# A state-space scan beside dilated attention on one core: output rows in pairs, the scan's weights built in pieces on two engines, K's weights loaded in halves, and a new written-out order

## The chip, the cores and the metric

The kernel runs on one core of a Trainium2 chip. A core has TensorE (PE; its weight loads are listed apart, as PEld), VectorE (DVE), ScalarE (ACT), GpSimd (POOL) and SyncE (SP), which here issues nearly all DMAs. The metric is the device time of one execution in microseconds, the median of several runs. Beside it stands one execution taken by the profiler, with its own time and its span from the first to the last instruction.

## The reference

Two independent parts work on inputs of 2048 tokens by 448 features in bf16, and their results are joined along the features to 2048 by 896. Cut to what is computed:

```
# part A: a diagonal linear recurrence (state-space layer), complex state of P = 448
Lam_bar = exp(exp(log_dt) * Lam);  B_bar = ((Lam_bar - 1) / Lam)[:, None] * Bmat
Bu = einsum("bld,pd->blp", x, B_bar)
h_t = Lam_bar * h_(t-1) + Bu_t                       # 2048 steps
y = 2 * einsum("blp,dp->bld", h, Cmat).real + x * Dskip
# part B: 16 heads of 28; each query sees 8 keys, 2 tokens apart, back in time
qkv = x @ wqkv
attn = softmax(q . k[pos - 2 w] * 28**-0.5, w = 0..7, masked before the start)
b = (sum_w attn_w * v[pos - 2 w]) @ wo
return concatenate([y, b], axis=-1)
```

## The kernel before, in words

**Layout.** A token is t = 16 p + j: p (0 to 127) is the partition or the column of a tile, j (0 to 15) picks the tile. All inputs x are brought in transposed by DMA (line 361 for part B, in `load_x` for part A), except that B's tokens 12 to 15 come plainly and are transposed by TensorE (`prep`, line 426), to have work early.

**Part B.** `prep` projects Q and K (lines 476 to 509) and evicts them from PSUM, `qk` multiplies q and shifted k on VectorE (lines 649 to 655) and sums heads on TensorE with 0/1 matrices (lines 666 and 672), `softmax` takes maximum, exponential, sum and normalizes. `v_proj` makes V (lines 755 and 762), whose evictions go to ScalarE (line 214) or VectorE (line 218). `pv` multiplies V by the attention and sums on VectorE in four groups of four tokens (lines 817, 820, 829, 832), then transposes and multiplies by wo (lines 857 to 900). For the last group (tokens 0 to 3) the sum of two halves is not made by VectorE: line 869 transposes both halves into one PSUM tile, 8 matmuls a token, and adds them there.

**Part A.** The state is handled as 7 blocks m of 64 complex entries. For each block `powers` builds 15 powers of the recurrence's 2x2 rotations as 128x128 matrices on VectorE (line 1182, one instruction of 128x1920). `scan` runs the recurrence of a block as a tree: first matmuls of x (lines 1232 and 1241) into four PSUM banks, ScalarE casts them to SBUF (L1250 or L1253), a matmul by a power adds them to the next bank (L1256), cast (L1260), and so on down to 64 columns (casts L1284, matmuls L1287 to L1294), then back up (L1301 to L1339). Each step of a block is a matmul that waits for a cast of ScalarE, and a cast that waits for a matmul; several blocks are interleaved. The carries of lines 1307 and 1308 are two matmuls each, of 128 and of 384 columns, since the last quarter of the state lies in a tile of its own. `outputs` gives y by seven matmuls a token over the blocks (line 1434), after four with Dskip (line 1430) for tokens 0 to 11; for tokens 12 to 15 VectorE multiplies x by Dskip (line 1411) and adds it in the eviction (line 1446).

**PSUM.** A pair of banks has the tag "W", six single banks the tag "s"; a matmul group that wants a bank waits until an eviction has freed it.

**The order.** Each step is a unit that is added to a `Planner` with its engine or a choice of two, a cost, and the units that it needs. If a list `ORDER` of the right length is there, the units are issued in just that order: an entry is the unit's number, and 1000 more when the second of its two engines is to do it. So the engine of each eviction, and the order on every engine, is written out by hand in that list; the costs only serve a search of it. Engines work strictly in their own order.

**DMA.** SP issues the loads in the order of the list: x of tokens 12 to 15 (line 345), K's weights (lines 338 and 340: rows 64 to 447, then the first 64 rows), Q's weights the same way, then the transposes. Output rows leave one token at a time (line 910 for attention, line 1449 for the state-space part), 32 transfers of 112 KB; rows for part B have four buffers (`yb`), those for part A eight (`ya`).

Of the kernel before, what the change touches and what calls it, by code (L numbers as in the profile page):

```python
# [9 lines left out]
ACT = mybir.ActivationFunctionType  # L10
# [22 lines left out]
QW = 2 + NCH  # L33
LV2 = ((1, 2, 3), (4, 8, 12), (16, 32, 48))
KPOW = sorted({1, 2, 4, 8, 12, 16} | {32 * k for ks in LV2 for k in ks})
# [5 lines left out]
FILL = (1, 3)  # L41
# [4 lines left out]
YG = ((3,), (7,), (11,), (1, 5), (9,), (0, 4), (8,), (2, 6), (10,), (12, 13), (14,), (15,))  # L46
YSPLIT = 8
ORDER = [
# [156 lines left out]
class Ctx:  # L205
# [83 lines left out]
    def warm(self):  # L289
# [5 lines left out]
        nc.vector.memset(z, 0.0)  # L295
        box = {}
# [10 lines left out]
    def late_tile(self):  # L307
        if self.late is None:
            self.late = self.rc
            self.ya_v = self.late[:, 8448:8448 + 3584].rearrange("p (r d) -> p r d", r=8)  # L310
            self.yb_v = self.late[:, 12032:12032 + 1792].rearrange("p (r d) -> p r d", r=4)
            self.ya_ring, self.yb_ring, self.ya_row = Ring(8), Ring(4), {}
        return self.late


class PartB:
# [7 lines left out]
    def loads(self):  # L324
# [11 lines left out]
        def wload(c0, c1):  # L336
            w = self.wqk[:, :, c0:c1] if c0 < 2 * D else self.wv
            nc.sync.dma_start(w[:, 1:4], self.B_wqkv[DT:D, c0:c1].rearrange("(k p) c -> p k c", p=NCH))
            for rows in ((slice(DT, NCH),) if c0 < 2 * D else (slice(0, DT), slice(DT, NCH))):
                nc.sync.dma_start(w[rows, 0], self.B_wqkv[0:DT, c0:c1])  # L340
        self.wload = wload
# [4 lines left out]
        wload(D, 2 * D)  # L346
        self.u_x3 = [P.add("ACTQ", 0.0, lambda: None, lat=t) for t in (3.45, 3.95)]
        self.u_w["K"] = P.add("ACTQ", 0.0, lambda: None, lat=6.2)

    def loads_more(self):  # L350
# [16 lines left out]
        u0 = self.u0 = P.add("SP", 2.35, lambda: None, lat=0.0)  # L367
        self.u_w["Q"] = P.add("SP", 1.0, lambda: self.wload(0, D), [u0], -1, lat=4.4)
# [8 lines left out]
    def load_v(self, deps):  # L377
        self.u_w[2] = self.plan.add("SP", 1.2, lambda: self.wload(2 * D, 3 * D), deps, 0.5, lat=3.5)
# [32 lines left out]
    def prep(self, u_warm):  # L411
# [6 lines left out]
        def xpose(j):  # L418
            box = {}

            def tr():
                pt = box["pt"] = self.psum.tile([NCH, 2, KT, NCH], bf16, name="pt_x", tag="s")
                for n in range(2):
# [3 lines left out]
            u = P.add("PE", 0.9, tr, [self.u_x3[(j - 12) // 2]], -8.5, acq="s")  # L427
# [24 lines left out]
        def banks(b, r, tiles, boxes, prio, rfirst):  # L452
# [5 lines left out]
            for kind, kt in tiles:  # L458
                wd.append(self.u_wm if kind == "M" else self.u_w[kind])
# [1111 lines left out]
```

## Time and profile before

| | us |
|---|---|
| median of 3 runs (lowest, highest) | 140.3 (139.42, 140.81) |
| the profiled execution's own time | 140.44 |
| its span | 138.7 |
| busy: TensorE, VectorE, ScalarE, GpSimd | 131.6, 123.8, 90.0, 17.7 |
| transfers of output rows | 32 of 112 KB, 1.8 from issue to landing (median) |
| granted clock of TensorE | 1.000 |

A row of the groups has the line, the engine, the operation, what it writes and reads, the shapes and the count, then the busy time and the mean duration in ns of one, then the idle time of the engine before them and what ended it. A row of a timeline has start, duration and the same names. A matmul's duration includes its way through the array; neighbours overlap, so what one costs is read from start to start. ScalarE's and VectorE's instructions overlap with the next one by about a tenth of a microsecond in the same way.

### The profile page before, as it was taken

How to read it: one execution, taken by the hardware profiler on the slowest of the kernel's cores; microseconds unless marked ns; L12 is line 12 of the kernel's file. 1: busy time of each engine (PE TensorE's matmuls, PEld its weight loads, DVE VectorE, ACT ScalarE, POOL GpSimd, SP SyncE). 2: the span in 40 equal slices, each digit the busy share in tenths (PEclk: the TensorE clock that was granted, in tenths of full speed). 3: DMA queues.
4: the chain of work that ended last, by engine and by line, in shares of the span. 5: the costliest groups of instructions: out<-in, count | busy, mean ns of one | idle time of the engine just before them, and what ended most of it. 6: DMA issues, size and time to landing. Idle time of an engine off the chain costs nothing.

```text
span 138.7 us, 2854 instructions
## 1 busy us (share of the span) xinstructions
PE 131.6 (95%) x1078; PEld 68.5 (49%) x1085; DVE 123.8 (89%) x136; ACT 90.0 (65%) x202; POOL 17.7 (13%) x69
## 2 busy tenths in 40 slices
PE   5999999999999999999999999999999999988990
PEld 1634435444555554756435564545655554534640
DVE  2268999899999999999999999999999999999820
ACT  3464589997563967776685998987637070722671
POOL 7489820028000000000000000000000000000000
PEclk9999999999999999999999999999999999999999
DMA  4979943645653349735898019000000827965774
GB/s 128 266 128 213 173 87 63 160 101 116 80 111 74 82 84 145 140 81 150 230 185 195 0 25 112 0 0 2 5 0 0 183 82 43 213 211 155 234 233 139
DMA packets 39582, 16.05 MB, mean 116 GB/s; under 512 B 31573, under 2 KB 38932, under 8 KB 39569
## 3 DMA queue, kind: packets, MB, share of 16 engines
q1 hardware_dynamic: 39506, 15.87, 54.0%
q8 instruction: 8, 0.13, 0.4%
q14 instruction: 5, 0.04, 0.1%
q10 hardware_dynamic: 63, 0.01, 0.0%
HBM read 4.32 MB, written 3.67 MB: 58 GB/s over the span
## 4 chain that ended last, share of the span: by engine, by line
DVE 35%; PE 31%; SPq 15%; issue 7%; DMA 6%; ACT 3%; DVEq 0%; ACTq 0%
DVE rb L820 13%; DVE prods L817 11%; SPq L361 8%; PE v_ps L762 7%; DVE rb L817 4%; PE qk_ps L476 4%; DMA out_dram<-qk 3%; PE logits L666 3%; PE y_ps L1434 3%; DMA rb<-in_B_x_dram 3%; DVE pw L1182 2%; DVE rb L829 2%; PE wo_ps L900 2%; PE scb L1232 2%; PE scp L1232 2%
## 5 line engine op out<-in xcount | busy, mean ns | idle before, releaser
L817 DVE TENSOR_TENSOR prods<-attn,vd 128x3584 bf16<-128x3584 bf16 x12 | 24.1, 2019 | 0.0
L820 DVE TENSOR_TENSOR rb<-rb,prods 128x3584 bf16<-128x3584 bf16 x11 | 22.2, 2021 | 0.1
L651 DVE TENSOR_TENSOR prods<-qk 128x3072 bf16<-128x3072 bf16 (+1 forms) x15 | 19.1, 1327 | 0.0
L214 ACT CAST qk<-wo_ps 128x448 bf16<-128x448 f32 (+1 forms) x16 | 8.3, 527 | 12.2 <-PE wo_ps L893 7.7
L1434 PE MATMUL y_ps<-Ccat,qk 128*128 128x448 bf16 x60 | 15.1, 352 | 0.1
L476 PE MATMUL qk_ps<-rb 128*128 128x512 bf16 x60 | 14.4, 379 | 0.0
L1434 PE MATMUL y_ps<-Ccat,h 128*128 128x448 bf16 x45 | 11.0, 352 | 0.9 <-ACT qk L214 0.9
L214 ACT CAST vd<-v_ps 128x448 bf16<-128x448 f32 x15 | 7.4, 539 | 5.8 <-PE v_ps L762 4.5
L1232 PE MATMUL scb<-xaT_sb,Bcat 128*128 128x512 bf16 x42 | 10.9, 380 | 0.0
L1232 PEld LDWEIGHTS <-Bcat 128*128 128x128 bf16 x84 | 7.6, 100 | 6.6 <-issue 0.4
L1284 ACT CAST ubuf<-scb 128x64 bf16<-128x64 f32 x35 | 7.1, 218 | 5.6 <-PE scb L1291 3.5
L762 PE MATMUL v_ps<-rb 128*128 128x448 bf16 x48 | 9.9, 353 | 0.0
L655 DVE TENSOR_TENSOR prods<-qk 128x768 bf16<-128x768 bf16 (+3 forms) x18 | 9.1, 569 | 0.3 <-ACT qk L214 0.2
L216 ACT ACTIVATE qk<-qk_ps 64x512 bf16<-64x512 f32 (+1 forms) x15 | 8.9, 599 | 0.6 <-PE qk_ps L509 0.3
L476 PEld LDWEIGHTS <-rb 128*128 128x128 bf16 x60 | 5.6, 98 | 7.1 <-DMA rb<-in_B_wqkv_dram 0.5
L1434 PEld LDWEIGHTS <-qk 128*128 128x128 bf16 x60 | 5.9, 98 | 5.3
L817 DVE TENSOR_TENSOR rb<-attn,vd 128x3584 bf16<-128x3584 bf16 x4 | 8.1, 2022 | 0.1
L893 PE MATMUL wo_ps<-wo_p,rb 128*128 128x448 bf16 x36 | 8.1, 354 | 0.0
L1182 DVE TENSOR_TENSOR pw<-Dm,spair 128x1920 bf16<-128x1920 bf16 x7 | 8.1, 1153 | 0.0
L214 ACT CAST qk<-qk_ps 128x512 bf16<-128x512 f32 (+2 forms) x11 | 6.3, 585 | 2.6 <-PE qk_ps L483 1.1
L1232 PE MATMUL scp<-xaT_sb,Bcat 128*128 128x512 bf16 x30 | 7.8, 380 | 0.0
L666 PE MATMUL logits<-prods,Zsel 128*32 128x256 bf16 x192 | 7.4, 274 | 0.0
(199 smaller groups left out, 261.9 us busy)
## 6 DMA issues: line engine op xcount, KB each, us to landing
out_dram<-qk SPq DMA_DIRECT2D x32, 112.0 KB, 1.8
vd<-vd SPq DMA_DIRECT2D x3, 392.0 KB, 4.7
rb<-in_B_wqkv_dram SPq DMA_DIRECT2D x3, 336.0 KB, 5.0
qk<-in_A_x_dram SPq DMA_DIRECT2D x1, 448.0 KB
ra<-in_A_B_re_dram SPq DMA_DIRECT2D x1, 392.0 KB, 4.3
ra<-in_A_B_im_dram SPq DMA_DIRECT2D x1, 392.0 KB, 5.9
rb<-in_A_C_re_dram SPq DMA_DIRECT2D x4, 98.0 KB, 2.9
rb<-in_A_C_im_dram SPq DMA_DIRECT2D x4, 98.0 KB, 2.8
```

Of the source, the lines that this page charges most:

```text
L214: nc.scalar.copy(out, in_)
L361: nc.sync.dma_start(self.xT[:, j], bass.AP(x.tensor, x.offset + j * D - DT, [[T * D, NCH], [1, KT * NCH]]), transpose=True)
L476: nc.tensor.matmul(out(n), lhsT=w(n, full, k), rhs=self.xT[:, j:j + 4, k, :], start=(not rfirst and k == 1), stop=(rfirst and k == KT - 1) ...
L651: V.tensor_tensor(out.rearrange("p i j k q -> p i (j k) q"), qq.unsqueeze(1).to_broadcast([NCH, 2, 4 * nk, NCH]), bass.AP(kk.tensor, kk.of ...
L655: V.tensor_tensor(jk(out[:, i, a:e]), qq, kk, op=ALU.mult)
L666: nc.tensor.matmul(lg[32 * i:32 * i + 32, 2 * tp:2 * tp + 2, :], lhsT=cx.Z[:, kt, zs], rhs=pr[:, :, i, kt, :], start=(new and kt == 0), st ...
L762: nc.tensor.matmul(box["ps"][:].rearrange("p h d -> p (h d)"), lhsT=self.xT[:, j, k, :], rhs=self.wv[:, k, :], start=False, stop=(k == KT ...
L817: V.tensor_tensor(tmp[i].rearrange("p (j d h) -> p j d h", j=8, d=DH), aa, self.vd[:, o:o + 8], op=ALU.mult)
L820: V.tensor_tensor(acc, acc, tmp[i], op=ALU.add)
L1182: V.tensor_tensor(t[:], self.o["Dm"][:].rearrange("p (a b) -> p a b", b=2).unsqueeze(1).to_broadcast([NCH, 2 * NPW, 32, 2]), self.sp[:, m ...
L1232: mt(box[i], lhsT=self.Bcat[:, k, m, :], rhs=self.xk(slice(i, None, 4), k), start=(i % 2 == 0 and k == 0), stop=False, **kw)
L1434: nc.tensor.matmul(ps, lhsT=h, rhs=self.Ccat[:, m, :], start=(m == 0 and not skip), stop=(m == NM - 1), skip_group_check=True)
```

## The change

1. *Powers in pieces.* The 15 powers of a block are built in four pieces (3, 4, 4 and 4 powers), each by VectorE in one instruction or by ScalarE in one ACTIVATE for each half of a power (128x64, the scale read per partition from a new f32 copy of the factors, which GpSimd makes). The scan's steps wait for their piece and not for all 15.
2. *Last sums joined by VectorE.* After each half of the last attention sum VectorE adds its two halves (128x896), and the transposes of tokens 0 to 3 are 4 matmuls each instead of 8.
3. *Output in pairs.* The 16 state-space rows leave in 8 transfers of two tokens, the attention rows of tokens 4 to 15 in 6; tokens 0 to 3 leave alone. Attention rows have six buffers. An attention pair is evicted in two casts behind each other. For tokens 0 to 3 the eviction can be ScalarE's or VectorE's.
4. *K's weights in halves.* The columns of K come in two transfers (256 and 192 columns, rows 64 to 447); the first 64 rows of K and Q together in one, issued by ScalarE. The first group of K's matmuls (tokens 12 to 15) is done in halves of two tokens as they come. Tokens 14 and 15 are transposed apart, and the warm-up has two matmuls less.
5. *Carries in one.* The tiles of the state are laid out so that the last quarter lies beside the others (132 columns each), and a carry is one matmul of 512 columns.
6. *The order.* 715 units instead of 687, in a new order, with other choices of engine.

The diff, cut to its core (the list to the lines that hold the first power pieces):

```diff
-FILL = (1, 3)
+FILL = (1, 1)
+PCUT = ((0, 3), (3, 7), (7, 11), (11, 15))
+MERGE = 1
+ADD = (0,0,0,0,0,0,0)
+OUTP = ((1, 5), (2, 6), (0, 4), (12, 13), (7, 11), (8, 9), (3, 10), (14, 15))
...
+    87, 88, 1079, 1093, 178, 1084, 138, 188, 179, 181, 273, 34, 1161, 1231, 97, 98, 110, 111, 112, 99, 102, 180,
...
+    127, 136, 128, 129, 175, 1125, 190, 196, 132, 546, 521, 522, 547, 549, 524, 186, 1233, 1357, 134, 548, 523, 550,
+    525, 133, 183, 187, 516, 541, 536, 542, 544, 537, 539, 517, 519, 191, 137, 184, 193, 1520, 1518, 1232, 1276,
+    1275, 545, 538, 540, 543, 185, 194, 192, 551, 531, 526, 552, 213, 527, 554, 529, 205, 214, 215, 553, 1315, 555,
...
-        wload(D, 2 * D)
+        for c0, c1 in ((D, D + 256), (D + 256, 2 * D)):
+            nc.sync.dma_start(self.wqk[:, 1:4, c0:c1], self.B_wqkv[DT:D, c0:c1].rearrange("(k p) c -> p k c", p=NCH))
...
+        nc.scalar.dma_start(self.wqk[DT:NCH, 0], self.B_wqkv[0:DT, 0:2 * D])
...
                         V.tensor_tensor(a, a, t, op=ALU.add)
+                        if MERGE:
+                            V.tensor_tensor(a[:, 0], a[:, 0], a[:, 1], op=ALU.add)
...
-                    for y in range(2):
+                    for y in range(2 - MERGE):
...
-                nc.sync.dma_start(self.out_b[:, j, :], cx.yb_v[:, jb["y"]])
+                if g:
+                    a, b = jb["mate"]["y"], jb["y"]
+                    nc.sync.dma_start(self.out_b[:, j - 1:j + 1, :], cx.yb_v[:, a:b + 1:b - a])
...
-        u = P.add("DVE", vec2(2 * NPW * PL), build, [self.u_s, *deps], prio, acq="pw")
+            n = 2 * (b - a)
+            if eng == "ACT":
+                for i in range(2 * a, 2 * b):
+                    nc.scalar.activation(t[:, i].rearrange("p a b -> p (a b)"), self.o["Dm"][:], ACT.Copy,
+                                         scale=self.spf[:, 2 * m * NPW + i:2 * m * NPW + i + 1])
+            else:
+                V.tensor_tensor(t[:, 2 * a:2 * b], self.o["Dm"][:].rearrange("p (a b) -> p a b", b=2).unsqueeze(1).to_broadcast(
+                    [NCH, n, 32, 2]),
...
+            us.append(P.add(("DVE", "ACT"), (vec2(n * PL), n * act(PL)), lambda eng, a=a, b=b: build(eng, a, b),
+                            [self.u_s, self.u_sf, *deps, *us[:1]], prio, acq=None if a else "pw"))
...
-            def carry(out, lt, Sc, hv):
-                mt(out[:, 0:NCH], lhsT=lt, rhs=Sc, start=False, stop=True, **kw)
-                mt(out[:, NCH:512], lhsT=lt, rhs=hv[:, 3, 0:384], start=False, stop=True, **kw)
...
+                mt(box[1].rearrange("p (g c) -> p g c", g=4), lhsT=L(2), rhs=hget()[1][:, :, 2:2 + NCH],
+                   start=False, stop=True, **kw)
...
-                nc.sync.dma_start(self.out_a[:, j, :], cx.ya_v[:, cx.ya_row[j]])
+                nc.sync.dma_start(self.out_a[:, a:b + 1:b - a, :], cx.ya_v[:, rows[a]:rows[b] + 1:rows[b] - rows[a]])
```

How the new list reads for what follows. The pieces of block m are units 231 to 234 (m = 0), 273 to 276 (1), 315 to 318 (2), 357 to 360 (3), 395 to 398 (4), 437 to 440 (5) and 477 to 480 (6). With 1000 more, so on ScalarE, stand 1231, 1232, 1233, 1274, 1275, 1276, 1315, 1316, 1317, 1357, 1358, 1360, 1395, 1477 and 1478; the other 13 are VectorE's. Those that begin a block (1231, 1315, 1357, 1395, 1477) are three powers, so 6 ACTIVATEs, the others 8.

ScalarE's own order from about the first piece to the scan's first cast is: piece 0 of block 0; the evictions of K and Q and of B's weights; pieces 2 of block 0 and 0 of block 3; two Q evictions with V of tokens 3, 10, 2 and 11 between them; pieces 1 of block 0, 3 and 2 of block 1; V of tokens 4, 7, 6, 5 and 1; piece 0 of block 2; V 0 and 12, the exponential, V 13, a copy; piece 1 of block 3; V 14; piece 1 of block 1; then the scan's first cast (L1253). Inside the scan stand 1316 (ahead of the 256-column cast of block 1), 1317, 1360 (ahead of that of block 2), 1395, 1477 and 1478.

In this stretch ten evictions and copies change from ScalarE to VectorE (a copy of B's weights, one of x, one Q and one K tile of 128 rows, one K tile of 64 rows, two tiles of the state's input weights, V of tokens 8, 9 and 15) and three from VectorE to ScalarE (a K tile of each half, V of token 1). Ahead of it three evictions of 64 rows go to VectorE and four of 128 rows to ScalarE. TensorE's order up to the scan's first dependent matmul has one group of three matmuls of block 1 behind it that was ahead of it.

More of the change, by code (lines that the diff above doesn't have):

```diff
@@ L295, in warm @@
         nc.vector.memset(z, 0.0)
+        self.first = self.pool.tile([NCH, 2], f32, name="first")
+        nc.vector.memset(self.first[:, 0:1], 0.0)
         box = {}
@@ L416, in prep, with xpose @@
         sc = DH ** -0.5
-        def xpose(j):
+        def xpose(j, nt):
             box = {}
             def tr():
-                pt = box["pt"] = self.psum.tile([NCH, 2, KT, NCH], bf16, name="pt_x", tag="s")
-                for n in range(2):
+                pt = box["pt"] = self.psum.tile([NCH, nt, KT, NCH], bf16, name="pt_x", tag="s")
+                for n in range(nt):
                     for k in range(KT):
@@ L491, in banks @@
                 res = ua, ub
+            elif j == 12 and tiles[0][0] == "K":
+                us = []
+                for a in (0, 2):
+                    for n in range(2):
+                        us.append(P.add("PE", pe(3, 256), lambda n=n, a=a: f(n, a, a + 2), x[a:a + 2] + wd + us[-1:], prio, acq=None if a else "s"))
+                u = P.add("PE", pe(1, 512), rr, [us[-1]] + dup, prio, mode="r")
+                us.append(u)
+                res = u, u
             else:
@@ L1327, in back, with fresh, s6, s7 @@
                 mt(box[2 * n], lhsT=cx.ident[:], rhs=box["eP"][:, n, :], start=True, stop=False, **kw)
[L1329 to L1333 removed]
+            def fresh(n, box=box, pair=pair):
+                if pair and n == 0:
+                    t = box["P"] = self.psum.tile([NCH, 2, 512], f32, name="scP", tag="W")
+                    box[0], box[2] = t[:, 0, :], t[:, 1, :]
+                elif not pair:
+                    box[2 * n] = self.psum.tile([NCH, 512], f32, name="scp%d" % (2 * n), tag="s")[:]
+            def s6(add=ADD[m] and not hold[0], fresh=fresh, box=box, L=L, hget=hget):
+                if add:
+                    fresh(0)
+                mt(box[0].rearrange("p (g c) -> p g c", g=4), lhsT=L(1), rhs=hget()[1][:, :, 2:2 + NCH],
+                   start=bool(add), stop=True, **kw)
+            def s7(add=ADD[m] and not hold[pair ^ 1], fresh=fresh, box=box, L=L, hget=hget):
+                if add:
+                    fresh(1)
+                mt(box[2], lhsT=L(1), rhs=hget()[0][:, 1, :], start=bool(add), stop=True, **kw)
             def evPf(box=box, hget=hget):
[L1336 removed]
+                nc.scalar.copy(hget()[0][:, 0::2, :], box["P"][:])
             def evpf(n, box=box, hget=hget):
[L1339 to L1340 removed]
+                nc.scalar.copy(hget()[0][:, 2 * n, :], box[2 * n])
+            dx = [self.u_bc[m], u_pads[m >= NHO]]
+            lw = lambda *ks: [u_pw[next(i for i, c in enumerate(PCUT) if PW[k] < c[1])] for k in ks]
             ux = lambda i: [self.u_x[j] for j in range(i, T, 4)]
@@ L1416, in outputs, with get @@
         nc, pool, P, cx = self.nc, self.pool, self.plan, self.cx
+        mate, rows, us_e, outs = {}, {}, {}, {}
+        for a, b in OUTP:
+            mate[a] = mate[b] = (a, b)
+            def get(a=a, b=b):
+                cx.late_tile()
+                rows[a], rows[b] = sorted(cx.ya_ring.get() for _ in range(2))
+            us_e[a, b] = [P.add("ACTQ", 0.0, get, self.u_h[4][:1], prio, acq=("ya", "ya"), lat=0.0)]
         for n, js in enumerate(YG):
@@ L1437, in ev @@
             def ev(eng, js=js, jb=jb):
-                cx.late_tile()
-                r = sorted(cx.ya_ring.get() for _ in js)
-                cx.ya_row.update(zip(js, r))
+                r = [rows[j] for j in js]
                 step = r[-1] - r[0] or 1
```

236 lines of the change are left out of this document (132 added, 104 removed), and 59 rows, old and new, of the table ORDER.

## The prediction

> **What bounds the kernel now.** I read the page first (busy time, then the chain that ended last), then busy time by stretch, then the timelines of the engines at the places that the change touches.
>
> ```profile
> PE 131.6 (95%) x1078; PEld 68.5 (49%) x1085; DVE 123.8 (89%) x136; ACT 90.0 (65%) x202; POOL 17.7 (13%) x69
> ...
> DVE 35%; PE 31%; SPq 15%; issue 7%; DMA 6%; ACT 3%; DVEq 0%; ACTq 0%
> ```
>
> ```profile
> 20.00:52.00 32.00, 31.97 (x334) 16.21 (x333) 30.96 (x41) 24.75 (x47) 3.75 (x6) 1.00 0.49 98
> 52.00:112.00 60.00, 59.32 (x510) 32.79 (x516) 59.62 (x44) 42.95 (x117) 0.00 (x0) 1.00 0.43 89
> ```
>
> The columns of the second fence are the stretch, its length, then busy us of PE, PEld, DVE, ACT and POOL, and the granted clock. TensorE and VectorE are both full from 20 to 112 us, with 0.03 and 1.0 us idle in the first stretch. ScalarE (ACT) is the only one with room: 7.25 us up to 52 and 17.05 us after. So work taken from TensorE or VectorE is worth up to its length, and work given to ScalarE is free only while it fits into these gaps in time for those who wait. ACT holds just 3% of the chain, but it empties the PSUM banks that TensorE needs (six of tag "s") and stands in every step of the scan.
>
> Where ScalarE's room lies ahead of the scan:
>
> ```profile
> 35.16 1.93 ACT L214 CAST vd<-v_ps 128x448 bf16<-128x448 f32 x4 [1.18 <-issue]
> 39.37 2.98 ACT L214 CAST vd<-v_ps 128x448 bf16<-128x448 f32 x6 [2.29 <-PE v_ps L762]
> 44.57 1.10 ACT L214 CAST vd<-v_ps 128x448 bf16<-128x448 f32 x2 [2.23 <-PE v_ps L762]
> ...
> 51.72 1.07 ACT L1253 CAST eP<-scp 128x512 bf16<-128x512 f32 x2 [1.02 <-PE scp L1241]
> ```
>
> ```profile
> 53.14 0.38 PE L1256 MATMUL scb<-eP,pw 128*128 128x512 bf16 x1
> ```
>
> The gaps of 1.18, 2.29, 2.23 and 1.02 us are pauses between groups of V evictions; the new power pieces are to go there. The scan begins with L1253 at 51.72, and its first dependent matmul (L1256) starts 1.42 us later.
>
> **The change, part by part.** The sum is made against the profiled execution's own 140.44 us (span 138.7 and 1.7 around it), 0.1 over the median of 140.3.
>
> *Powers.* Seven VectorE instructions become 28 pieces. By the new order list 15 of them (five of 6 instructions, ten of 8, so 110) go to ScalarE as one ACTIVATE of 128x64 with a per-partition scale; 13 stay on VectorE. The nearest rows for such an ACTIVATE:
>
> ```profile
> L1137 ACT ACTIVATE Dg<-ident,dsk x4: 392/398/414, 82.6 to 83.5; 128x128 bf16<-128x128 bf16 x4
> ```
>
> ```profile
> 86.95 0.29 ACT L1297 CAST S<-scb 128x128 bf16<-128x128 f32 x1
> 87.14 0.37 ACT L1270 CAST eA<-scb 128x256 bf16<-128x256 f32 x1
> ...
> 91.07 0.21 ACT L1284 CAST ubuf<-scb 128x64 bf16<-128x64 f32 x1 [0.65 <-PE scb L1291]
> 91.18 0.54 ACT L214 CAST qk<-wo_ps 128x448 bf16<-128x448 f32 x1
> ```
>
> The four of L1137 have the same form (SBUF to SBUF, scale by pointer) at twice the width and start 0.30 us apart. A plain cast holds ScalarE for 0.19 us at 128 columns (86.95 to 87.14) and 0.11 at 64 (91.07 to 91.18). So the new ones lie between 0.11 and 0.30; I take 0.30 less the 0.06 to 0.08 that half the width saves, 0.24, near the row that shares the form. A piece of eight then holds ScalarE for 1.9 us; the planner books 0.87.
>
> The Trainium skill's page "ScalarE: Activation LUTs", section "What ACT_TABLE_LOAD costs", gives 186 ns plus 0.833 ns per column, 93 ns more for each pointer operand, and 93 ns of overlap between neighbours: an estimate of 0.239 us by that page, which leaves the sum at 144.5; without its pointer term it would be 0.146 and the pieces would fit, 138.2. The trace agrees with the term: 386 ns for L1137 by the page, 398 measured.
>
> *ScalarE up to the scan.* Nine pieces (66 ACTIVATEs) stand ahead of the scan's first cast: 66 x 0.24 = 15.8 us. Ten evictions and copies of this stretch move from ScalarE to VectorE and three come back. By the pair at 51.72 (0.49 apart at 512 columns) that is some 4.6 us less and 1.4 more. Of the 24.75 us of the row, 24.5 lie before 51.72. So ScalarE needs 24.5 + 15.8 - 4.6 + 1.4 = 37.1 us in 31.7: 5.4 too many. I take off 0.6 (tails of 0.1 us that overlap once the six gaps are filled) and 0.4 for an earlier start (below): the scan's first cast comes 4.4 us late, at about 56.1, and L1256 0.6 us after it, at 56.7, instead of 53.14. TensorE has by then done 0.65 us less (one group of three matmuls moved behind). So it is 3.56 + 0.65 = **4.2 us behind**, and since it was full before, nothing behind absorbs that. What waits, in order: three pieces in a row (24 ACTIVATEs, 5.7 us) stand in front of four V evictions, where the gap was 2.3; TensorE's V matmuls wait for banks, then the mask and VectorE's maximum behind it, then the scan. Ends: 0 if all pieces find gaps, 8.2 if each ACTIVATE takes 0.30 (66 x 0.06 = 4.0 more).
>
> *ScalarE in the scan.* Six more pieces (44 ACTIVATEs, 10.5 us) fit the 17 us of room, but each is one block in a chain that goes to and fro between ScalarE and TensorE. Counting by the new order what TensorE has queued during each block: at m=2, piece 1 (ahead of s1's 256-column cast) it has two groups of sums, some 0.9 us, against 1.9; at m=3, piece 3 (ahead of s2's), 1.5 us of scan matmuls against 1.9 and a cast. So 1.0 + 0.7 = **1.7 us**; the other four are hidden behind more than their length. Ends 0 and 10.5.
>
> *VectorE.*
>
> ```profile
> 20.37 1.15 DVE L1182 TENSOR_TENSOR pw<-Dm,spair 128x1920 bf16<-128x1920 bf16 x1
> 21.43 0.62 DVE L1130 TENSOR_TENSOR Gd<-Dm,gs 128x896 bf16<-128x896 bf16 x1
> 21.97 1.15 DVE L1182 TENSOR_TENSOR pw<-Dm,spair 128x1920 bf16<-128x1920 bf16 x1
> ```
>
> ```profile
> L655 DVE TENSOR_TENSOR prods<-qk 128x512 bf16<-128x512 bf16 x2 | 0.8, 422 | 0.0
> L218 DVE CAST qk<-qk_ps 128x512 bf16<-128x512 f32 x5 | 3.3, 685 | 0.4 <-PE qk_ps L483 0.4
> ```
>
> A whole power holds VectorE for 1.06 us (20.37 to 21.43), a piece of 512 columns for about 0.33 (422 ns less the 0.09 that such rows overlap), one of 384 for 0.27. So -7 x 1.06 + 11 x 0.33 + 2 x 0.27 = -3.2 us. An eviction holds it for 0.60 (685 less 0.09): six of 512 columns and one V leave (-4.1), eight of 512, three V and two copies come (+6.8). The two new sums of halves are 128x896, 0.54 each by the row at 21.43: +1.1. Net +0.6 us, with the last sums at its end.
>
> *The tail.*
>
> ```profile
> 126.52 2.10 DVE L832 TENSOR_TENSOR rb<-rb,prods 128x1792 bf16<-128x1792 bf16 x2
> ```
>
> ```profile
> 129.82 1.50 PE L869 MATMUL pt_o<-ident,rb 128*128 128x128 bf16 x24
> ```
>
> ```profile
> 132.44 0.45 PE pt_o L869 x8
> ```
>
> VectorE's last sum ends at 128.62; TensorE comes to it at 129.82. Half of the 32 transposing matmuls go: 16 x 0.45 / 8 = **-0.9 us**. The 1.1 us of new sums lie in the 1.2 us of that wait while TensorE is no earlier than now; without that cover they cost up to 1.1.
>
> *Output rows.*
>
> ```profile
> PE y_ps L1434 <- ACT qk L214: 0.9, 1, 0.9
> ...
> ACT qk L214 <- DMA out_dram<-qk: 2.7, 2, 2.3
> ```
>
> ```profile
> 120.24 5.35 SPq L1449 DMA_DIRECT2D out_dram<-qk  x2
> ```
>
> Issues fall from 32 to 18. The waits of the tail quoted here end with landings and evictions, not with an issue, so SP's shorter queue counts 0. Attention rows now have six buffers, not four, so the two waits of ScalarE for a landing (2.7 us) go, and with them TensorE's only long idle: **-0.9 us**. If the stall of SP at 120.24 comes again behind the big load of x, this stays: ends -0.9 and 0. A pair leaves when its second row is ready; the rows that end the kernel still leave alone or are early, 0.
>
> *Start.*
>
> ```profile
> 1.26 1.89 PE L302 MATMUL warm_ps<-prods 128*128 128x512 bf16 x4 [1.26 <-DVE prods L295]
> ...
> 5.96 0.82 PE L302 MATMUL warm_ps<-prods 128*128 128x512 bf16 x3
> 6.82 1.47 PE L476 MATMUL qk_ps<-rb 128*128 128x512 bf16 x6
> 8.13 1.03 PE L509 MATMUL qk_ps<-rb 128*128 128x512 bf16 x4
> ```
>
> ```profile
> 2.22 0.58 SPq L340 DMA_DIRECT2D rb<-in_B_wqkv_dram  x1
> ```
>
> The first half of K's weights lets L476 begin before 6.82, but L509 needs Q's weights, which are the same bytes behind it. One such issue of K's (0.58) and one of Q's leave SP for one on ScalarE's queue, so Q's main part and the transposes behind it are issued some 0.6 us and more earlier, while the second half of K adds one. Ends 0 and 0.8; I take **0.4**, already counted above. Two warm-up matmuls less lie in waiting time: 0.
>
> *Carries.* Two matmuls (128 and 384 columns) become one of 512, 14 times.
>
> ```profile
> 102.93 0.22 PE L1307 MATMUL scb<-S,pw 128*128 128x128 bf16 x1
> 102.99 0.33 PE L1308 MATMUL scb<-qk,pw 128*128 128x384 bf16 x1
> 103.15 0.54 PE L1434 MATMUL y_ps<-Ccat,qk 128*128 128x448 bf16 x2
> ```
>
> The pair holds TensorE for 0.22 us (102.93 to 103.15), and a group of three 512s at 5.96 moves on in 0.22 each: 0, at best 0.4 in all. POOL's new cast and memsets come when it is idle (3.75 us busy of 32): 0.
>
> Sum: 140.4 + 4.2 + 1.7 - 0.9 - 0.9 = **144.5 us**, slower by 3%.
>
> **Rivals.** About 1% (138.9 to 141.7) is what a measurement of this kernel can tell from no change.
>
> *The pieces fit (faster).* ScalarE's need up to 51.7 us is 21.3 + 66x; it fits while x is under 0.157 us. The plain cast of 64 columns (0.11) lies below that, the pointer ACTIVATE of 128 (0.30) above. If it fits, 140.4 - 0.9 - 0.9 - 0.4 = 138.2. For it: the gaps of 2.29 and 2.23 us. Against it: L1137's 0.30.
>
> *VectorE takes over (no change).* ScalarE keeps up, but TensorE comes to the last sums at 129.82 - 0.4 - 0.9 = 128.5, while VectorE, +0.6 us, ends at 129.2 less an earlier start; the sums then stand in the path for up to 1.1 us: 138.2 + 1.1 = 139.3. For it: VectorE is full in both rows. Against: it needs the first rival to hold.
>
> *TensorE's clock falls (slower still).* While TensorE waits, its clock may be cut. The first four matmuls ran 0.42 us apart ((1.89 - 0.63) / 3), those at 5.96 0.22 apart, so it starts at half speed and had recovered 4.7 us later. One such stretch loses 4.7 / 2 = 2.35: 146.9. Against it: the waits I expect are 0.7 to 4 us and split. The Trainium skill's page "TensorE: Matmul & The Clock Gate", Part 1, puts the half rate behind an idle window of about 3.4 us and the return behind a busy one; no row after 5.96 here shows a drop, the longest idle being 0.9 us.
>
> **How the numbers follow.** My forecast 0.60 (own range 142.0 to 147.6: the lateness between 3.0 and 5.5, the scan's between 0.4 and 3.5); the clock 0.06; the pieces fit 0.22; VectorE 0.12. Slower by over 1%: 0.66; within 1%: 0.12; faster: 0.22. The range reaches from 137.8 (the start's other end, 138.2 - 0.4) to 148.
>
> **What would show it.** Right: 110 ACTIVATEs from Dm some 0.24 us apart, ScalarE busy about 113 us, the first eP cast near 56, TensorE idle ahead of v_ps and of scb, put down to ACT. The tail: 16 pt_o matmuls, no wait for a landing in ScalarE. Wrong: ACTIVATEs 0.15 apart or less, or a first eP cast at or before 52 with TensorE full; then the sum loses 5.9. If TensorE is late by more than ScalarE's blocks, something that I left at 0 (the transposes' new order, the paired rows) has failed.

## The result and the profile after

The kernel after takes 149.68 us (median of 4 runs, 148.90 to 150.82), the kernel before on the same chip 139.86 (4 runs, 138.87 to 140.81). The ratio is 1.071, 95% interval 1.0603 to 1.0817: slower, by more than the forecast's 144.5 us and outside its range of 137.8 to 148.0. The profiled execution of after took 150.82 us, the longest of its four, with a span of 149.2. The ratios leave out executions over 1.5% above the fastest of their kernel, among them one of 224.6 us at a granted clock of 0.574.

First the page of after (the busy line and its costliest group), then its busy time in the two stretches that were shown of before.

```profile
PE 135.6 (91%) x1053; PEld 68.8 (46%) x1059; DVE 126.2 (85%) x154; ACT 110.3 (74%) x305; POOL 17.5 (12%) x76
...
L1234 ACT ACTIVATE pw<-Dm,spf 128x64 bf16<-128x64 bf16 x110 | 27.6, 345 | 0.0
```

```profile
20.00:52.00 32.00, 30.30 (x278) 14.58 (x277) 28.27 (x42) 29.98 (x87) 1.62 (x2) 1.00 0.61 99
52.00:112.00 60.00, 53.81 (x473) 27.79 (x477) 55.97 (x53) 53.57 (x171) 1.38 (x6) 1.00 0.41 82
```

TensorE is no longer full: it is idle for 1.70 us in the first stretch and 6.19 in the second (before 0.03 and 0.68). VectorE has 3.73 and 4.03 us of room, and ScalarE, which had 7.25 and 17.05, has 2.02 and 6.43. The 110 ACTIVATEs are the largest group of the page.

ScalarE's timeline of after ahead of the scan, where before had gaps:

```profile
34.28 3.44 ACT L1234 ACTIVATE pw<-Dm,spf 128x64 bf16<-128x64 bf16 x14
...
40.28 5.84 ACT L1234 ACTIVATE pw<-Dm,spf 128x64 bf16<-128x64 bf16 x24
46.00 1.82 ACT L220 CAST vd<-v_ps 128x448 bf16<-128x448 f32 x4
48.92 0.53 ACT L220 CAST vd<-v_ps 128x448 bf16<-128x448 f32 x1 [1.11 <-PE logits L291]
...
55.15 2.02 ACT L1234 ACTIVATE pw<-Dm,spf 128x64 bf16<-128x64 bf16 x8
57.07 0.51 ACT L220 CAST vd<-v_ps 128x448 bf16<-128x448 f32 x1
57.48 2.02 ACT L1234 ACTIVATE pw<-Dm,spf 128x64 bf16<-128x64 bf16 x8
59.40 1.05 ACT L1310 CAST eP<-scp 128x512 bf16<-128x512 f32 x2
```

Fourteen ACTIVATEs take 3.44 us and one of them 0.34, so they start 0.24 apart, as forecast. The four gaps of before are gone, and from 28 us on ScalarE goes from one block to the next but for one wait of 1.11 us for TensorE, at 48.92. The scan's first cast (L1310, before L1253) comes at 59.40 and not at 51.72; the forecast had 56.1.

TensorE's timeline of after in the same place:

```profile
38.26 2.04 PE L779 MATMUL v_ps<-rb 64*128 64x448 bf16 x5
...
46.58 1.63 PE L779 MATMUL v_ps<-rb 64*128 64x448 bf16 x5 [0.45 <-ACT vd L220]
...
60.02 0.86 PE L1313 MATMUL scb<-eP,pw 128*128 128x512 bf16 x2 [0.61 <-ACT eP L1310]
```

Much of the loss ahead of the scan hardly shows as idle time. The V matmuls of L779 follow each other some 0.4 us apart, as fast as ScalarE frees banks, but each lasts 0.35, so TensorE counts as busy. With faster ACTIVATEs (below) five of them take 0.92 us and not 2.04.

To compare kernels I use three lengths, read from TensorE's rows: up to its first matmul with Q's weights (L509 of before, 8.13; L533 of after, 9.99), from there to the scan's first dependent matmul (L1256, 53.14; L1313, 60.02), and from there to the end of its last matmul (135.15; 145.77). They add up to the whole difference: 10.62 us, beside 10.5 in the spans.

| kernel (profiled execution) | start | to the scan | scan to end |
|---|---|---|---|
| before | 8.13 | 45.01 | 82.01 |
| after | 9.99 | 50.03 | 85.75 |
| difference | +1.86 | +5.02 | +3.74 |
| by the forecast | -0.4 | +3.95 | +0.55 |
| all pieces with an immediate | 8.71 | 44.88 | 82.43 |
| only the nine ahead of the scan | 8.40 | 45.59 | 85.48 |
| only the six in the scan | 9.10 | 50.02 | 82.33 |
| two warm-up matmuls more | 10.47 | 50.02 | 85.71 |
| one immediate ACTIVATE a piece | 9.21 | 45.00 | 82.73 |
| pieces on GpSimd | 8.76 | 50.83 | 84.19 |
| pieces on VectorE | 9.17 | 45.88 | 108.12 |
| the same, one piece moved | 8.43 | 45.88 | 85.47 |
| before, sums and six buffers | 7.99 | 45.59 | 81.32 |
| before, six buffers alone | 8.04 | 45.05 | 80.71 |

(The forecast's row: L1256 at 56.7 less a start at 7.73 is 3.95 more than 45.01; behind it 0.65 of moved matmuls + 1.7 - 0.9 - 0.9.)

These are lengths of single executions. Up to the scan the kernel with immediates in all pieces and the one with immediates in the first nine have the same instructions, and their lengths there differ by 0.71 us; those of the last two rows differ by 0.54. Less than that can't be read from one row.

### The profile page after: what moved, and what is told of

Same layout as the page of the kernel before. It is cut to its first block, busy times and chain, and to the rows that moved or that the text cites. A ratio compares the mean times of both kernels' runs of the same rounds, so it can differ in the third digit from the quotient of the medians.

```text
span 149.2 us, 2907 instructions
## 1 busy us (share of the span) xinstructions
PE 135.6 (91%) x1053; PEld 68.8 (46%) x1059; DVE 126.2 (85%) x154; ACT 110.3 (74%) x305; POOL 17.5 (12%) x76
## 5 line engine op out<-in xcount | busy, mean ns | idle before, releaser
L1234 ACT ACTIVATE pw<-Dm,spf 128x64 bf16<-128x64 bf16 x110 | 27.6, 345 | 0.0
L492 PE MATMUL qk_ps<-rb 128*128 128x512 bf16 (+1 forms) x66 | 16.3, 393 | 0.0
L1520 PE MATMUL y_ps<-Ccat,qk 128*128 128x448 bf16 x64 | 16.0, 352 | 0.1
L220 ACT CAST qk<-wo_ps 128x448 bf16<-128x448 f32 x14 | 7.3, 545 | 8.1 <-PE wo_ps L919 6.6
L222 ACT ACTIVATE qk<-qk_ps 128x512 bf16<-128x512 f32 (+1 forms) x14 | 8.1, 594 | 5.1 <-PE qk_ps L533 5.0
L1520 PE MATMUL y_ps<-Ccat,h 128*128 128x448 bf16 x48 | 11.7, 353 | 0.0
L220 ACT CAST qk<-y_ps 128x448 bf16<-128x448 f32 (+1 forms) x9 | 5.8, 665 | 6.5 <-PE y_ps L1520 5.4
L492 PEld LDWEIGHTS <-rb 128*128 128x128 bf16 x66 | 7.0, 109 | 7.1 <-issue 0.6
L1341 ACT CAST ubuf<-scb 128x64 bf16<-128x64 f32 x35 | 7.6, 230 | 3.2 <-PE scb L1344 1.6
L1348 PEld LDWEIGHTS <-pw 128*128 128x128 bf16 x63 | 4.7, 106 | 6.3 <-issue 4.0
```

Source lines behind the costliest of these rows:

```text
L220: nc.scalar.copy(out, in_)
L222: nc.scalar.mul(out, in_, scale)
L492: nc.tensor.matmul(out(n)[:, a:e], lhsT=w(n, full, k), rhs=self.xT[:, j + a:j + e, k, :], start=(not rfirst and k == 1 and a == 0), stop=( ...
L1234: nc.scalar.activation(t[:, i].rearrange("p a b -> p (a b)"), self.o["Dm"][:], ACT.Copy, scale=self.spf[:, 2 * m * NPW + i:2 * m * NPW + i ...
L1520: nc.tensor.matmul(ps, lhsT=h, rhs=self.Ccat[:, m, :], start=(m == 0 and not skip), stop=(m == NM - 1), skip_group_check=True)
```

## The experiments

**The price of the pointer.** Theory: ScalarE's overload is the loss, and all of it hangs on the 0.24 us of an ACTIVATE whose scale is read from memory. Rival: something else of the change (the order, the start, the pairs) costs most. Three kernels with an immediate scale, in all pieces or in part of them; their powers hold other values.

```diff
-                                         scale=self.spf[:, 2 * m * NPW + i:2 * m * NPW + i + 1])
+                                         scale=0.5)
```

> The changed kernel with an immediate scale of 0.5 in all 110 ACTIVATEs of the powers on ScalarE, in place of the per-partition pointer (so these powers hold other values); order, engines and waits stay. Theory S (ScalarE is overloaded by the length of these instructions): they start 0.15 us apart instead of 0.24, ScalarE has 10.2 us less to do, the first eP cast moves from 59.4 to about 53.5, and the time falls from 149.7 to about 142 (140 to 144). Rival O (the new order and its choice of engines are bad by themselves, whatever an ACTIVATE lasts): 147.5 or more.

> The same for the nine pieces (66 ACTIVATEs) ahead of the scan alone. Theory S: 6.1 us less for ScalarE there, the first eP cast at about 54, the time about 144.5 (143 to 146). Rival O: 148 or more. If the lateness ahead of the scan is given back inside it (the scan is bound by its own blocks), 147 and the scan's stretch grows by what the first one loses.

> The same for the six pieces (44 ACTIVATEs) inside the scan alone. Theory S: 4.1 us less for ScalarE in the scan; TensorE's idle there (13.0 us against 8.1 before) falls by about 2.5, the time about 147 (145.5 to 148). Rival O: 149 or more.

Measured: all 141.07 us (10 runs; ratio to before 1.0096, 1.0055 to 1.0137); only the nine ahead of the scan 144.58 (1.0346, 1.0286 to 1.0406); only the six in the scan 147.00 (1.0532, 1.0452 to 1.0612). Before took 140.0 on that chip. The rows of the kernel with immediates everywhere, first the tile's instructions on ScalarE, then TensorE's timeline:

```profile
L1234 ACT ACTIVATE pw<-Dm x110: 238/247/289, 20.7 to 92.9; 128x64 bf16<-128x64 bf16 x110
```

```profile
36.60 0.92 PE L779 MATMUL v_ps<-rb 64*128 64x448 bf16 x5
...
53.59 0.38 PE L1313 MATMUL scb<-eP,pw 128*128 128x512 bf16 x1
```

Nothing has changed but the form and value of the operand, and the 7.1% over before are 1.0%: 8.6 us are gone. An ACTIVATE lasts 247 ns (median) where after has 339, and they start 0.146 apart, not 0.24. That is below the 0.157 at which the forecast's faster rival was to decide, and the pieces do fit: the stretch to the scan is back at 44.88. Pointers ahead of the scan cost 147.00 - 141.07 = 5.9 us, where 66 x 0.094 = 6.2 would be their whole extra length; pointers in the scan cost 3.5, of 44 x 0.094 = 4.1. Taken from after instead, the two are 149.68 - 144.58 = 5.1 and 149.68 - 147.00 = 2.7; the truth lies between, since 5.9 and 3.5 make 9.4 and both together are worth 8.6. So most of the extra isn't hidden in either place. The Trainium skill's page "ScalarE: Activation LUTs", section "What ACT_TABLE_LOAD costs", has 93 ns for each pointer operand; these two kernels, 92 ns apart, agree.

Which pieces of the scan wait is seen where pointers stand only there. TensorE's waits of that kernel from 54 us to the end of the scan:

```profile
PE scb L1330 <- ACT eA L1327: 1.3, 2, 0.6
PE scb L1348 <- ACT ubuf L1341: 0.9, 1, 0.9
PE scb L1367 <- ACT h L1362: 0.7, 1, 0.7
PE scp L1400 <- ACT h L1374: 0.7, 1, 0.7
PE scb L1344 <- ACT ubuf L1341: 0.5, 1, 0.5
```

Six waits, one behind each of the six pieces, 4.1 us in all; with immediates none of them is there, and in after all six stand with the same lengths. The forecast had two of the six wait.

**Lighter still.** One immediate ACTIVATE of 128x512 (or 384) for each piece, 634 ns in the median.

```diff
-                for i in range(2 * a, 2 * b):
-                    nc.scalar.activation(t[:, i].rearrange("p a b -> p (a b)"), self.o["Dm"][:], ACT.Copy,
-                                         scale=self.spf[:, 2 * m * NPW + i:2 * m * NPW + i + 1])
+                nc.scalar.activation(t[:, 2 * a:2 * b].rearrange("p n a b -> p n (a b)"),
+                                     self.o["Dm"][:].unsqueeze(1).to_broadcast([NCH, n, PL]), ACT.Copy, scale=0.5)
```

> The changed kernel with one ACTIVATE with an immediate scale for each of ScalarE's fifteen pieces (128x384 or 128x512 out of a repeated Dm; these powers hold other values): about 0.5 us a piece, 7 us in all where the immediate scale left 16 and the change has 26.5. If the 1% that the kernel with the immediate scale lacks against before is still ScalarE, the time falls to 139 (138.3 to 139.8); if it is the new order, the start or VectorE's added work, it stays at 141 (140.3 to 141.7).

Measured: 141.92 us (9 runs; 1.0093, 1.0057 to 1.0128), beside before's 140.28. That is 0.2 above the expected range, but the ratio is that of the kernel with 110 immediates. Half the load again gains nothing, so what is left of the loss isn't ScalarE's. TensorE's timeline of this kernel at its end, and VectorE's:

```profile
131.61 0.39 PE L895 MATMUL pt_o<-ident,rb 128*128 128x128 bf16 x4
133.31 0.38 PE L895 MATMUL pt_o<-ident,rb 128*128 128x128 bf16 x4 [1.31 <-DVE qk L1529]
```

```profile
130.81 0.62 DVE L858 TENSOR_TENSOR rb<-rb 128x896 bf16<-128x896 bf16 x1
131.36 1.08 DVE L1487 TENSOR_TENSOR qk<-qk,rb 128x1792 bf16<-128x1792 bf16 x1
132.63 2.15 DVE L1529 TENSOR_TENSOR qk<-y_ps,qk 128x448 bf16<-128x448 f32 x3 [0.19 <-ACT rb L900]
```

TensorE stands 1.31 us for VectorE, which comes late through its two new sums (L858) and what it does behind them. That is the forecast's second rival: once ScalarE keeps up, VectorE ends last.

**The start.** after comes to Q's weights 1.86 us late. Theory F: the two warm-up matmuls that were taken away; rival P: the moment at which TensorE comes to full speed, which differs from run to run.

```diff
-FILL = (1, 1)
+FILL = (1, 3)
```

> The changed kernel with the two warm-up matmuls back (FILL 1, 3). In its trace TensorE reached full speed only at about 9.7 us, in the one of before at 5.9. Theory F (the missing warm-up matmuls leave TensorE too idle for its clock to rise): full speed near 6, the time 1.8 lower, about 147.9. Rival P (the moment differs from run to run by itself): full speed anywhere between 6 and 10 in this trace and in those of the three other kernels, which share the changed kernel's start; the time within 1 of 149.7.

Measured: 151.1 us (1.0797, 1.0726 to 1.0867). Two more warm-up matmuls gain nothing here, and rival P misses as well, by a little (1.4 us from 149.7, where it allowed 1). But this kernel doesn't bring the old start back: there three warm-up matmuls stand at 5.96 us, ahead of K's first ones, here they come at 8.08, behind nine of them. So F is shown to fail for that place only. TensorE's timeline of after, then that of the kernel with immediates ahead of the scan only, whose instructions are the same up to there:

```profile
5.99 2.13 PE L492 MATMUL qk_ps<-rb 128*128 128x256 bf16 x9
...
8.34 1.82 PE L492 MATMUL qk_ps<-rb 128*128 128x256 bf16 x6
9.99 1.03 PE L533 MATMUL qk_ps<-rb 128*128 128x512 bf16 x4
```

```profile
6.09 1.16 PE L492 MATMUL qk_ps<-rb 128*128 128x256 bf16 x9 [0.35 <-DMA rb<-in_B_wqkv_dram]
...
7.30 1.26 PE L492 MATMUL qk_ps<-rb 128*128 128x256 bf16 x6
8.40 1.03 PE L533 MATMUL qk_ps<-rb 128*128 128x512 bf16 x4
```

The same nine matmuls take 2.13 us or 1.16: half speed to 9.70 us in one, to 5.01 in the other, by the first rise of the clock that the trace records; the spacing of the matmuls agrees. Even at full speed (second fence) Q's weights come 0.27 us later than in before: twelve of K's matmuls of 256 columns, three of 512 and a warm-up, 2.3 us of TensorE, now stand ahead of them, and the halves of K let the first begin only 0.73 us earlier (6.09, before 6.82). In the nine traces with the new start Q's first matmul comes between 8.40 and 10.47 us, in the three with the old one between 7.99 and 8.13. So the new start is later in every trace, never earlier, and with the pointers the delay reaches the scan whole: behind it three kernels with all nine pointer pieces have 50.02 or 50.03 us. The clock rises between 4.90 and 9.70 us with the new start and between 5.47 and 6.22 with the old one. Three traces are too few to say that the old start is always early, and what sets the moment (the start's own work, chance, or both) stays open. The Trainium skill's page "TensorE: Matmul & The Clock Gate", Part 1, has a free-running window of about 3.4 us, and so a transition that varies by some 0.5 us; these traces vary by 4.8.

**Another engine for the pieces.** If ScalarE has no room for the pieces, has another engine? First VectorE: all 28 pieces there, at the same places of the list (15 numbers of the list lose their 1000; the first is shown).

```diff
-    87, 88, 1079, 1093, 178, 1084, 138, 188, 179, 181, 273, 34, 1161, 1231, 97, 98, 110, 111, 112, 99, 102, 180,
+    87, 88, 1079, 1093, 178, 1084, 138, 188, 179, 181, 273, 34, 1161, 231, 97, 98, 110, 111, 112, 99, 102, 180,
...
```

> The changed kernel with all 28 pieces of powers on VectorE, the fifteen of ScalarE at the same places of the list. Theory S (the pieces are only a question of who has room): ScalarE's lateness goes (first eP cast at 53 to 54), but VectorE, full before the change, carries 4.7 us more (5 x 0.27 + 10 x 0.33) on top of the 0.6 of the change; less 1.2 us of room in front of the last transposes that is some 4 us over before: 144 (142.5 to 146). Rival D (VectorE had room in the changed kernel, 23 us idle): 141 as with the immediate scale.

Measured: 168.33 us (1.2013, 1.1955 to 1.2072), far off. Up to the scan it goes as expected (45.88). Then, TensorE's timeline and VectorE's:

```profile
100.04 0.53 PE L911 MATMUL wo_ps<-wo_p,rb 64*128 64x448 bf16 x2
123.88 0.29 PE L1337 MATMUL scb<-eB,pw 128*128 128x128 bf16 x1 [23.31 <-DVE pw L1237]
```

```profile
101.03 0.42 DVE L1237 TENSOR_TENSOR pw<-Dm,spair 128x512 bf16<-128x512 bf16 x1
101.37 2.02 DVE L844 TENSOR_TENSOR rb<-rb,prods 128x3584 bf16<-128x3584 bf16 x1
...
121.47 2.02 DVE L841 TENSOR_TENSOR prods<-attn,vd 128x3584 bf16<-128x3584 bf16 x1
123.40 0.42 DVE L1237 TENSOR_TENSOR pw<-Dm,spair 128x512 bf16<-128x512 bf16 x1
```

TensorE waits 23.31 us for one piece of 0.42 us. VectorE runs some 20 us behind TensorE here, which costs nothing as long as only the end needs its sums. The second piece of block 6 stands on VectorE behind twelve large products and sums, a good place for ScalarE and 22 us too late for VectorE. The next kernel moves this one unit.

```diff
-    571, 602, 603, 561, 604, 605, 606, 451, 452, 599, 422, 453, 600, 481, 454, 482, 423, 455, 456, 457, 483, 458,
-    478, 487, 459, 424, 460, 425, 485, 461, 484, 426, 486, 462, 488, 463, 427, 464, 428, 489, 490, 465, 429, 491,
+    478, 571, 602, 603, 561, 604, 605, 606, 451, 452, 599, 422, 453, 600, 481, 454, 482, 423, 455, 456, 457, 483, 458,
+    487, 459, 424, 460, 425, 485, 461, 484, 426, 486, 462, 488, 463, 427, 464, 428, 489, 490, 465, 429, 491,
```

> The kernel after with all 28 pieces of powers on VectorE, and one of them, the second piece of block 6, moved ahead in the list from behind the products of the next 22 us to ahead of the piece of products that stood before them; nothing else is changed against the run with all pieces on VectorE (168.3 us, span 166.5). There TensorE stood 23.3 us for that one piece of 0.42 us, which VectorE had in its queue behind eleven large products. Theory (the place, not the load): that wait goes, with some 2 us of half-speed matmuls behind it. VectorE itself stood without a gap from 54 us to 135.0 us, so its last sum can't be ready much earlier than 135.0, and TensorE has 5.1 us of work behind that, the rest of the span 3.3 us and 1.5 us lie around it: 145 us (144 to 146). Rival (VectorE can't carry the pieces): TensorE's waits for powers come up elsewhere in the scan, and the time stays at 150 us or above.

Measured: 144.81 us (1.0303, 1.0270 to 1.0336): the place it was; of the waits for powers 1.5 us are left. What holds it at 144.8 is VectorE, full to its last sum; its row and the wait of TensorE behind it:

```profile
133.65 0.62 DVE L858 TENSOR_TENSOR rb<-rb 128x896 bf16<-128x896 bf16 x1
```

```profile
136.15 0.38 PE L895 MATMUL pt_o<-ident,rb 128*128 128x128 bf16 x4 [0.69 <-DVE qk L1530]
```

So VectorE has no room for them either. GpSimd had, by after's page: 12% busy.

```diff
-            us.append(P.add(("DVE", "ACT"), (vec2(n * PL), n * act(PL)), lambda eng, a=a, b=b: build(eng, a, b),
+            us.append(P.add(("DVE", "POOL"), (vec2(n * PL), n * act(PL)), lambda eng, a=a, b=b: build(eng, a, b),
```

> The changed kernel with ScalarE's fifteen pieces on GpSimd, as multiplications like VectorE's, at the same places of the list; GpSimd is idle from 30 us on. By L1124 (210 columns in 0.56 us) a piece takes some 1.3 us. Theory S: as good as the immediate scale, 140.5 (139.5 to 141.5). Rival G (GpSimd's multiplications hold up VectorE's, which then last longer than 2.02 us for 128x3584): 142 or more.

Measured: 148.82 us (1.0615, 1.0571 to 1.0658). The expectation fails, on the rival's side. VectorE's group of the 1536-column products, of after and then of this kernel:

```profile
L673 DVE TENSOR_TENSOR prods<-qk 128x1536 bf16<-128x1536 bf16 x6 | 5.5, 955 | 0.0
```

```profile
L673 DVE TENSOR_TENSOR prods<-qk 128x1536 bf16<-128x1536 bf16 x6 | 8.0, 1371 | 0.0
```

And the pieces themselves, from the view of the tile, with GpSimd's timeline:

```profile
L1234 POOL TENSOR_TENSOR pw<-Dm,spair x15: 828/1035/2152, 17.3 to 89.4; 128x512 bf16<-128x512 bf16 x10, 128x384 bf16<-128x384 bf16 x5
```

```profile
17.26 9.38 POOL L1234 TENSOR_TENSOR pw<-Dm,spair 128x384 bf16<-128x384 bf16 x7
...
27.67 5.04 POOL L1234 TENSOR_TENSOR pw<-Dm,spair 128x512 bf16<-128x512 bf16 x5
```

Between 17 and 33 us GpSimd multiplies with one pause of 1 us, and VectorE's products take 1371 ns in the mean and not 955: the four that run beside GpSimd 1.18 to 1.80 us, the two behind it still 0.95. A copy of VectorE (64x512) that lasts 0.29 us with the pieces on VectorE lasts 2.72 there. GpSimd's own pieces reach 2152 ns. TensorE waits 1.64 us up to 23.18 and 2.18 up to 27.27, and its granted clock then falls to half for 3.41 us. The stretch to the scan is 50.83 us, as long as with the pointers; how much of that is the slower VectorE and how much the clock wasn't separated. The Trainium skill's "GPSIMD Engine Reference", section "1. Specifications", says that the two engines share their access to SBUF and contend where VectorE reads two inputs; this trace agrees.

**The tail.** The forecast gave 0.9 us to the sums on VectorE and 0.9 to the six buffers. Both alone, in the kernel before with its old order:

```diff
+                        V.tensor_tensor(a[:, 0], a[:, 0], a[:, 1], op=ALU.add)
...
-                    for y in range(2):
+                    for y in range(1):
...
-            self.ya_ring, self.yb_ring, self.ya_row = Ring(8), Ring(4), {}
+            self.ya_ring, self.yb_ring, self.ya_row = Ring(8), Ring(6), {}
```

> The kernel before with two parts of the change alone: VectorE joins the last sums (16 transposing matmuls less), and attention rows have six buffers; order and units as before. The prediction's terms: -0.9 and -0.9, 138.2 where before is 140.0. Rival: VectorE's two sums (1.1 us) stand in the path and take the first back, 139.3; or the stall of the output queue comes again and takes the second, 139.1; both, 140.2.

Measured: 140.24 us (12 runs; 0.9996, 0.9966 to 1.0027): nothing. TensorE's wait and VectorE's rows in that kernel:

```profile
PE pt_o L870 <- DVE rb L833: 0.9, 1, 0.9
```

```profile
128.08 0.62 DVE L833 TENSOR_TENSOR rb<-rb 128x896 bf16<-128x896 bf16 x1
128.62 1.08 DVE L832 TENSOR_TENSOR rb<-rb,prods 128x1792 bf16<-128x1792 bf16 x1
129.74 0.62 DVE L833 TENSOR_TENSOR rb<-rb 128x896 bf16<-128x896 bf16 x1
```

The wait for a landing at 125.28 is gone, and TensorE reaches the transposes at 129.21, but VectorE's last sum is done at 130.36. Its two rows of L833 hold VectorE for some 0.54 us each. Part of its lateness is older, though: it came to its last products (L832) at 126.95, 0.43 us later than before did, and that was lost ahead of the tail, where this kernel's instructions are those of before. So the buffers without the sums:

```diff
-            self.ya_ring, self.yb_ring, self.ya_row = Ring(8), Ring(4), {}
+            self.ya_ring, self.yb_ring, self.ya_row = Ring(8), Ring(6), {}
```

> The kernel before with six row buffers of the attention output in place of four and nothing else (the last sums stay on TensorE, the order is the same). With both the buffers and the sums on VectorE the time was 140.24 us against 140.28: the wait of 0.89 us for the landing of a row at 125.28 us was gone, and TensorE stood 0.88 us for VectorE's last sum at 130.42 us instead. Theory: the landing wait is worth its 0.9 us less what VectorE's last product sum (done at 128.6 us in the profile of before, when TensorE could come to its transposes at 129.2 us at the earliest) takes back, which is nothing; so 139.6 us (139.3 to 139.9), and the sums on VectorE are what took the gain back. Rival: the tail is bound by VectorE whatever the buffers are, 140.2 us, no change.

Measured: 139.47 us (8 runs; 0.9922, 0.9896 to 0.9948) where before took 140.57: faster by 0.8%, a little, but the interval leaves out no change. TensorE's timeline and VectorE's:

```profile
127.50 1.49 PE L1434 MATMUL y_ps<-Ccat,S 128*128 128x448 bf16 x7
128.83 1.50 PE L869 MATMUL pt_o<-ident,rb 128*128 128x128 bf16 x24
```

```profile
126.47 2.09 DVE L832 TENSOR_TENSOR rb<-rb,prods 128x1792 bf16<-128x1792 bf16 x2
```

VectorE is done at 128.56, 0.27 us ahead of TensorE: 32 transposes and no wait beat 16 with one. Behind the scan's first dependent matmul the buffers alone gain 1.30 us (80.71 beside 82.01), and the sums take 0.61 of that back (81.32); that nothing at all is left is what the times say, not these rows. This is the only kernel of the study that beats the one before.

## Why the forecast was right in kind and wrong in size

By the three lengths the forecast was off by 2.3 us at the start, 1.1 up to the scan and 3.2 behind it.

- **The price of an ACTIVATE** (0.24): right, 0.24 apart, 345 ns in the mean. ScalarE is busy 110.3 us where I said about 113.
- **Up to the scan** (4.2 behind): the mechanism was right, the size too small. The first cast came 7.7 us late (1.86 of it from the start) and not 4.4. ScalarE's load was as summed: its rows from 20 us to that cast hold 37.3 us, the sum had 37.1. What failed is the 1.0 us taken off (0.6 for tails that overlap, 0.4 for an earlier start), and ScalarE's own waits, which the sum has at nothing once the gaps are filled: it stood for 2.1 of those 39.4 us, 1.11 of them at 48.92. TensorE's length grew by 5.02 us with 0.65 us of matmuls moved out of it, so it lost 5.7.
- **Start** (-0.4): wrong in sign. +1.86 in this trace and later in all nine; I had looked at when weights are issued, and neither at how fast TensorE runs when they come nor at the longer work that the new order puts ahead of Q.
- **In the scan** (1.7, four of six pieces "hidden behind more than their length"): failed, and it is the largest miss (2.4 us). All six show up as waits of TensorE, 4.1 us in all, and pointers alone are worth 2.7 to 3.5 us there against immediates. An immediate piece of eight (1.2 us) does find cover: with all of them the length to the end is 82.43, beside 82.01 before. One of 1.9 doesn't. I had counted what TensorE has queued in the list's order, as if ScalarE came to each block on time.
- **Merge** (-0.9) and **landing** (-0.9): the landing wait went as said, and the buffers are worth 0.8% alone. The merge was costed with the 1.2 us by which TensorE came behind VectorE's last sum in before as its cover, but the buffers use up that same time; two gains were counted on one cover. In before's order their times cancel. In after TensorE is late, so its times can't tell them apart.
- **VectorE +0.6, hidden**: too small, and hidden only in part. VectorE is busy 2.4 us longer than before in after and 1.8 with immediates, and even in after TensorE waits 0.5 us for it at the end. With ScalarE relieved VectorE holds TensorE for 0.9 to 1.3 us at the end, which is one reason why the kernel whose pieces fit took 141.07 us and not the 138.2 of that rival; its start, 0.58 us later than before's, is another.
- **The clock falls** (146.9): not during the waits of after's profiled execution; its granted clock is 1.00 in both stretches, and its six waits in the scan are 0.5 to 0.9 us each. With the pieces on GpSimd waits of 1.64 and 2.18 us were enough, so this rival was nearer than the forecast's "0.7 to 4 us and split" made it. Half speed did cost in after, but at the start.

Of the 9.8 us between the medians, the pointers are 8.6 (the ratios 1.071 and 1.0096, times 140), shown by changing the operand alone. The other 1.3 are what a kernel with pieces that fit still lacks; in its profile the start (0.58) and the end (0.42) are longer than before's, by no more than single lengths vary. The profiled execution of after is 1.1 us above its median, so part of its late start may be its own.

## What to carry to other kernels

Work moved into an engine's gaps is free only up to a threshold, and beyond it most of the excess is paid (5.1 to 5.9 us of 6.2 ahead of the scan): work out the price at which the gaps are full (0.157 us here) and take the instruction's form, above all an operand by pointer, as part of the price. Two savings that rely on the same wait of another engine are one saving, so after each step ask which engine is now last. A place in an order list belongs to the engine it was found for: when a unit changes its engine, see how far that engine runs behind the one that waits.

## What the runs showed of the hardware

- A per-partition scale makes an ACTIVATE of 64 columns 92 ns longer (339 against 247), and its neighbours start that much further apart.
- When TensorE stood still for 23 us (pieces on VectorE), its granted clock went to half and came back. Busy time by stretch, of that kernel; the clock is the third figure from the end:

```profile
100.00:102.00 2.00, 0.56 (x3) 0.10 (x2) 2.00 (x3) 0.41 (x2) 0.00 (x0) 1.00 0.00 0
102.00:104.00 2.00, 0.00 (x0) 0.00 (x0) 1.97 (x2) 0.00 (x0) 0.00 (x0) 0.83 0.00 0
104.00:106.00 2.00, 0.00 (x0) 0.00 (x0) 1.91 (x2) 0.00 (x0) 0.00 (x0) 0.50 0.11 23
...
124.00:126.00 2.00, 2.00 (x8) 0.93 (x8) 2.00 (x2) 0.68 (x3) 0.00 (x0) 0.50 0.00 0
126.00:128.00 2.00, 2.00 (x16) 1.22 (x15) 2.00 (x2) 0.93 (x3) 0.00 (x0) 0.69 0.02 4
```

The last matmul ended at 100.57. A mean of 0.83 over 2 us is 0.68 us at half, so it fell at about 103.3, 2.7 us later; by the 0.69 it came back at about 127.2, 3.4 us after the first matmul at 123.88. The trace's record of the clock has 103.34 and 127.23. So long a stop isn't needed: with the pieces on GpSimd the clock went to half at 27.54, when TensorE had been busy for 1.24 of the last 3.41 us, and came back at 30.95. In the profiled execution of after it didn't fall.
- In these traces the changes of the clock lie whole multiples of 3.41 us apart: 95.57 and 23.89 with the pieces on VectorE (28 and 7 times), 20.48 and 3.41 with GpSimd (6 times and once). The first one comes at another moment in each trace, between 4.90 and 9.70 us.
- At the start of after the matmuls run at half speed (2.13 us for nine) while the granted clock of the first 10 us stands at 1.00, since the trace's record of the clock begins only at 9.70: there the spacing of the rows tells more than that column.
- VectorE and GpSimd slow each other when both multiply two operands: VectorE's 128x1536 goes from 955 ns to as much as 1.80 us, GpSimd's 128x512 from 1.03 (beside VectorE's casts) to 1.76.
